# Second MLP product of the first two row chunks as seven block products, with the sums of the second weight matrix formed earlier

## The chip, the cores and the metric

The kernel runs on one NeuronCore of a Trainium2 chip. The engines that matter are PE (TensorE, matrix products), DVE (VectorE), ACT (ScalarE), POOL (GpSimd, which also issues a queue of DMA transfers) and SP (SyncE, which issues another). The metric is the device time of one execution in microseconds (us); lower is better. One execution was profiled, and its trace is what the times below are read from.

## The reference, cut to what matters

The program is an attention block followed by a Fourier mix with an MLP. Batch is 4, heads 8, sequence 768, head dimension 64.

```python
scores = scale * np.matmul(q, k.transpose(0, 1, 3, 2)) + bias   # bias: -slope * distance
scores = np.where(keep, scores, -1e9)                           # 8 global keys, 96 local keys
a = softmax(scores)
x = (a @ v) as (4, 768, 512)

X = np.fft.fft(np.fft.fft(x, axis=1), axis=2)
u = x + np.real(X)
un = (u - mean(u)) / np.sqrt(var(u) + 1e-6)
out = u + np.maximum(un @ w_ch1, 0.0) @ w_ch2                   # w_ch1 512x2048, w_ch2 2048x512
```

The change concerns the last product, `relu(...) @ w_ch2`. Its inner dimension is 2048 and its output has 512 columns.

## The kernel before, in words

**Tiling and stages.** The 3072 rows of the output are cut into twelve chunks of 256 rows, three to a batch: chunks 0, 1 and 2 are batch 0, and so on. For each batch the program does attention (scores `sc`, exponentials `ex`, the product with v, `pav`), divides by the row sums on DVE (`norm` at line 860, which writes the attention output `X[b]`), folds the sequence and the features with additions on DVE (`fold_s` and `fold_d`, lines 927 and 1086), does the remaining Fourier products on PE (`py`, `pu`), and adds and normalises on DVE and ACT (`u`, `un`). A chunk's normalised rows are transposed (`unT`; chunks 0 to 2 by PE as `ptu`, the others by DMA), then come eight groups of products with the first weight matrix (`ph`, eight matrix instructions each, line 1378), a ReLU into the hidden tile `hT` by ACT or DVE, and the second product.

**The second product, two forms.** Chunks 0 and 1 use `pg_unit` (line 1573): for each of the chunk's two blocks of 128 rows, sixteen matrix instructions of 512 columns add up in one PSUM bank `pg`, in four parts of four; DVE then multiplies by the row's 1/std and adds to `u` (line 1594). Chunks 2 to 11 use `pg_units` (line 1688): the 256 rows by 2048 inner by 512 columns are seen as 2x2 blocks times 2x2 blocks, and seven block products take the place of eight. A block product is eight matrix instructions of 256 columns (line 1697). They are issued as five pieces: p1 (one product), p45 (two), p6 (one), p7 (one) and p32 (two); the last chunk has six. p45 needs the first sum of the hidden tile, p6 the second, p7 the third and p32 the fourth. These four sums are made by DVE in `s_sums` (lines 1661, 1667, 1664 and 1672). Each piece is followed by one addition into `u` on DVE (line 1715), so a chunk has five of these where `pg_unit` has two.

**The sums of the second weight matrix.** The seven products also need sums of blocks of `w_ch2`, called W2T(0) to W2T(3). DVE makes them in `w2_sums` (line 1628), for i = 0 and 1, each with half the rows: `one` makes W2T(1) in the tile `misc` (line 1633), and `rest` makes W2T(3) in place, over a block of the weights themselves (line 1637), and then W2T(0) and W2T(2) in a tile `tt` (lines 1638, 1639). For i = 0 they read the first and third quarter of the weight rows, for i = 1 the second and fourth. Because W2T(3) overwrites weights that `pg_unit` reads, `rest` waits until chunks 0 and 1 are done (`pgdone`). The tile `tt` is also where batch 1's attention output stands (`XT`, line 837), so `rest` waits for that too. The constant `CS = 2` (line 410) says from which chunk on `pg_units` is used.

**Loads.** The weights come by eight transfers of 512 KB on POOL's queue, four for each matrix (`wload`, line 1883). The same queue loads q, k and v. Transfers of this queue use eight completion semaphores in turn, named DMASW0 to DMASW7 in the order rows below.

**What sets the order.** Each engine works through its instructions in program order. The order is written out by hand in the table `ORDER` (line 261), one list for each engine, of names such as G4 (a unit of the second product), H3 (a group of `ph`), M14 (a unit of the mix) or A43 (a unit of attention). A planner, `Plan`, walks these lists and issues the instructions; its `later` (line 87) records what an operation needs. The semaphore waits in the program follow from the tiles that are read and written. An operation whose input isn't there yet holds up all that stands behind it on its engine.

Of the kernel before, what the change touches and what calls it, by code (L numbers as in the profile page):

```python
# [12 lines left out]
ALU = mybir.AluOpType  # L13
# [11 lines left out]
class Plan:  # L25
# [135 lines left out]
    SHARED = {"kB": 1, "vB": 1, "sid": 1, "f1": 0, "f2": 0, "f3": 0, "z": 0, "g0": 0, "w": 0, "s": 0, "su": 0, "w2a": 0, "w2t": 0, "ex": 0}  # L161
# [78 lines left out]
    def unit_start(self, unit):  # L240
# [7 lines left out]
        if not there:  # L248
# [23 lines left out]
        ),  # L272
        "ACT": (
# [10 lines left out]
        ),  # L284
        "DVE": (
# [20 lines left out]
        ),  # L306
        "SP": (
            "T.6 T.0 T.9 T.127 T.35 T.133 T.10 T.128 G7.1 T.91 T.134 T.136 G3.1 T.137 T.130 T.100 T.131 T.101 T.176 T.182 T.102 T.177 T.185 T.34 T.206 "
            "T.183 T.140 T.186 T.212 T.205 T.211 T.179 T.149 T.180 T.263 T.150 T.151 T.222 T.223 T.228 T.189 T.229 T.198 T.199 T.200 T.245 T.239 T.240 "
            "T.246 T.258 T.256 T.257 "  # L310
        ),
    }
# [71 lines left out]
def kernel(  # L384
# [13 lines left out]
    Dm = H * Dh  # L398
# [1612 lines left out]
```

## Time and profile before

| | |
|---|---|
| time, median of 3 runs | 245.23 us (243.34, 245.23, 246.89) |
| the profiled execution | 244.25 us, of which 242.4 us lie between its first and last instruction (the span) |
| PE, matrix instructions | busy 230.6 us of the span, 3026 instructions |
| DVE | busy 206.4 us, 463 instructions |
| ACT | busy 143.3 us |
| POOL | busy 115.7 us |
| granted TensorE clock | 1.000 |

The 1.85 us between the profiled time and its span lie ahead of the first and behind the last instruction that was profiled. "PE" rows are matrix instructions and "PEld" rows the loads of their stationary operand, which overlap them. A row of the timeline gives the start, the duration, the engine, the line and operation, the tiles (written from read), how many, and in brackets how long the engine had been idle and what ended it. Durations of matrix instructions overlap, since they are pipelined: the start of one to the start of the next tells what a group costs.

### The profile page before, as it was taken

The page shows a single profiled execution, that of the slowest core. Times are in us where ns is not written, and L with a number is a line of the kernel's source. Part 1 is how long each engine was busy: PE and PEld are TensorE (multiplying, and loading weights), DVE is VectorE, ACT ScalarE, POOL GpSimd, SP SyncE. Part 2 cuts the span into 40 slices and gives each one's busy share as a digit, 9 for nine tenths or more (in the row PEclk, how much of TensorE's full clock was granted, in tenths as well). Part 3 has the DMA queues.
Part 4 walks back from the last instruction along what each step waited for, and adds up shares of the span by engine and source line. Part 5 has one row for each costly group of instructions (what it writes and reads, how often), then busy time and mean ns, then how long its engine had stood idle before and what let it go on. Part 6 is the DMA issues. An engine that isn't in the chain of part 4 may idle for free.

```text
span 242.4 us, 7226 instructions
## 1 busy us (share of the span) xinstructions
PE 230.6 (95%) x3026; PEld 188.2 (78%) x3026; DVE 206.4 (85%) x463; ACT 143.3 (59%) x233; POOL 115.7 (48%) x161
## 2 busy tenths in 40 slices
PE   7898899899999999889999999999999999999993
PEld 3465677598677668678988888898889899888882
DVE  3478997979961898999999899999998899988992
ACT  2288469974127978665268848845754588376300
POOL 8998769975800319999029854104140350003020
PEclk9999999999999999999999999999999999999999
DMA  7999999999999998999999956964892363103003
GB/s 181 166 164 180 203 209 193 206 207 168 129 159 178 206 182 66 136 178 96 133 220 294 200 76 192 177 32 87 252 271 46 78 141 66 25 0 143 34 26 147
DMA packets 103248, 35.44 MB, mean 146 GB/s; under 512 B 91088, under 2 KB 98640, under 8 KB 103216
## 3 DMA queue, kind: packets, MB, share of 16 engines
q0 software_dynamic: 72448, 19.16, 78.1%
q1 hardware_dynamic: 27216, 13.08, 25.6%
q10 hardware_dynamic: 3552, 2.75, 4.6%
q8 instruction: 23, 0.38, 0.6%
q14 instruction: 9, 0.07, 0.1%
HBM read 31.44 MB, written 8.65 MB: 165 GB/s over the span
## 4 chain that ended last, share of the span: by engine, by line
PE 77%; DVE 12%; ACT 4%; DMA 3%; issue 2%; POOL 1%; DVEq 0%; SPq 0%; POOLq 0%
PE ph L1378 22%; PE pgD L1697 14%; PE pgA L1697 10%; PE phA L1471 4%; PE py L1139 4%; PE pav L856 4%; PE pg L1583 4%; PE phX L1471 3%; DMA qkT<-qk 3%; ACT ex L800 3%; PE pu L1226 3%; PE pz L1860 2%; DVE x L868 2%; DVE ex L812 2%; PE sc L771 2%
## 5 line engine op out<-in xcount | busy, mean ns | idle before, releaser
L1378 PE MATMUL ph<-unT,w 128*128 128x256 f16 x576 | 71.4, 273 | 0.0
L1378 PEld LDWEIGHTS <-w 128*128 128x128 f16 x576 | 55.2, 98 | 8.4
L1383 ACT ACTIVATE hT<-ph 128x512 f16<-128x512 f32 x63 | 36.9, 596 | 41.7 <-PE ph L1378 41.4
L1697 PEld LDWEIGHTS <-hT 128*128 128x128 f16 x288 | 27.8, 98 | 4.8 <-issue 1.4
L797 ACT ACTIVATE er<-sc 128x1024 f16<-128x1024 f32 (+1 forms) x24 | 22.2, 951 | 10.0 <-DVE ex L812 6.0
L800 ACT ACTIVATE ex<-sc 128x1024 f16<-128x1024 f32 (+1 forms) x24 | 21.4, 959 | 8.5 <-PE sc L739 8.5
L1329 POOL TENSOR_SCALAR sm<-sm 128x2 f32<-128x2 f32 x12 | 5.2, 432 | 42.2 <-ACT un L1322 41.6
L1568 POOL DMA_INDIRECT out_dram<-u,back x4 | 5.4, 1345 | 30.7 <-DVE u L1715 30.4
L569 POOL DMA_DIRECT2D qk<-in_k_dram x16 | 13.5, 845 | 12.6 <-DMA qkT<-qk 8.4
L1715 DVE SCALAR_TENSOR_TENSOR u<-pgA,sm,u 128x256 f32<-128x256 f32 (+1 forms) x30 | 16.9, 565 | 1.5 <-PE pgA L1697 1.4
L1715 DVE SCALAR_TENSOR_TENSOR u<-pgD,sm,u 128x512 f32<-128x512 f32 (+1 forms) x21 | 15.0, 719 | 2.6 <-PE pgD L1697 2.5
L812 DVE TENSOR_TENSOR ex<-er,mk 128x1024 f16<-128x1024 f16 (+1 forms) x24 | 16.1, 688 | 0.0
L1583 PE MATMUL pg<-w,hT 128*128 128x512 f16 x64 | 15.5, 379 | 0.0
L1322 ACT ACTIVATE un<-un 128x512 f16<-128x512 f16 x24 | 15.0, 629 | 0.5 <-DMA unT<-un 0.5
L856 PE MATMUL pav<-v,ex 128*128 128x65 f16 x224 | 13.1, 193 | 1.9 <-DVE x L868 1.1
L856 PEld LDWEIGHTS <-ex 128*128 128x128 f16 x352 | 12.7, 97 | 2.8 <-issue 1.1
L569 POOL DMA_DIRECT2D qk<-in_q_dram x16 | 13.9, 879 | 0.0
L1152 ACT ACTIVATE zy<-py 128x1024 f16<-128x1024 f32 (+1 forms) x13 | 10.7, 825 | 4.3 <-PE py L1139 4.2
L868 DVE TENSOR_TENSOR x<-pav,rc 128x384 f16<-128x384 f32 x24 | 12.6, 554 | 0.6
L1384 DVE TENSOR_SCALAR hT<-ph 128x512 f16<-128x512 f32 x9 | 6.2, 685 | 7.1 <-PE ph L1378 7.0
L624 ACT ACTIVATE qk<-phA 128x512 f32<-128x512 f32 x12 | 6.9, 595 | 7.8 <-PE phA L1471 7.8
L1139 PE MATMUL py<-t,ww 128*128 128x256 f16 x80 | 11.2, 273 | 0.0
(217 smaller groups left out, 563.8 us busy)
## 6 DMA issues: line engine op xcount, KB each, us to landing
w<-in_moe_w_ch_dram POOLq DMA_DIRECT2D x8, 512.0 KB, 11.4
out_dram<-u SPq DMA_DIRECT2D x15, 256.0 KB, 3.5
v<-in_v_dram POOLq DMA_DIRECT2D x16, 192.0 KB, 7.0
qk<-in_k_dram POOLq DMA_DIRECT2D x16, 96.0 KB, 4.9
qk<-in_q_dram POOLq DMA_DIRECT2D x16, 96.0 KB, 5.0
xr<-xd SPq DMA_DIRECT2D x3, 512.0 KB, 4.0
xd<-x ACTq DMA_DIRECT2D x2, 768.0 KB, 5.3
ex<-w POOLq DMA_DIRECT2D x3, 512.0 KB, 6.7
```

The lines of the kernel that those rows point to most:

```text
L569: nc.gpsimd.dma_start(qk16[n][:, w, :, h], src[b, h0 + h].rearrange("(i m) d -> m i d", m=P))
L797: A(mine(), cut(pa), AF.Exp, 0.0, 0.125)
L800: A(cut(expst[hp][:, :, g * 512:g * 512 + (384 if g == 2 else 512)]), cut(pa), AF.Exp, 0.0, 0.125)
L812: VT(o, mine(), m, op=ALU.mult)
L856: nc.tensor.matmul(o[:, s * 65:(s + 1) * 65], lhsT, w, start=(a == 0), stop=(a == len(ops) - 1), skip_group_check=True)
L868: VT(X[b][:, 3 * (k.start + h):3 * (k.start + h) + 3, 2 * hp * Dh:(2 * hp + 2) * Dh].rearrange("p y (h d) -> p y h d", d=Dh), pv[:, h, :, ...
L1139: nc.tensor.matmul(o, lhsT, rhs, start=(x == 0), stop=(x == len(ops) - 1))
L1378: nc.tensor.matmul(ph[:, a * CH:(a + 1) * CH].rearrange("p (x m) -> p x m", x=2), W1[0][:, d, jb * P:(jb + 1) * P], UNT[c][:, :, d, :], st ...
L1383: pl.later([("ACT", act(512), lambda: A(dst, ph, AF.Relu)), ("DVE", dve(512), lambda: V.tensor_scalar_max(dst, ph, 0.0))], [], e, [("h", c ...
L1583: nc.tensor.matmul(pg, HT[c][:, jb, t * P:(t + 1) * P], W2[0][:, jb, :], start=(jb == 0), stop=(jb == NJ - 1))
L1697: nc.tensor.matmul(o, lhs(j), rhs(j), start=(first and j == 0), stop=(j == NK - 1), skip_group_check=True)
L1715: V.scalar_tensor_tensor(o, x, r(t), acc, op0=ALU.mult, op1=ALU.add)
```

## The change

Chunks 0 and 1 take the form with seven block products as well (`CS = 0`). Three things come with it.

- `w2_sums` is regrouped into three steps: `one` makes W2T(1), `middle` makes W2T(0) and W2T(2) from W2T(1) and unchanged weights, and `rest` makes W2T(3) in place. The eight additions are as many and as large as before. Nothing waits for `pgdone` any more, since no chunk reads the plain block.
- Batch 1's attention output stands in the tile `x`, where batch 0's stood, and the tile `tt` is free for the weight sums once the first loads of q and k that pass through it are used.
- The order table is new for all five engines. In it five ReLUs of `ph`, five normalisations `un`, three copies of transposed q and k (`qkT`) and two of `unT` go from DVE to ACT, and three of POOL's key copies (`kB`, in the tile `mk`) to DVE.

```diff
@@ Plan
-    SHARED = {... "w2a": 0, "w2t": 0, "ex": 0}
+    SHARED = {... "w2a": 0, "w2b": 0, "w2t": 0, "ex": 0}
@@ Plan.ORDER, "PE"
-... A44 H5 H4 A42 H1 A43 H6 M11 H0 H7 M13 G4 G0 H13 G5 G6 H9 H14 G1 G7 G2 H8 ...
+... A44 H3 A42 H7 A43 H6 H5 H4 M11 H2 H1 H0 H15 H12 H9 H8 G0 H10 H14 M13 H13 G1 M14 G2 H11 M15 G3 M18 G4 ...
@@
-    CS = 2
+    CS = 0
@@ w2_sums
+        def middle():
+            VT(W2T(0)[:, k0], W2[0][:, k0, 0:HC], W2T(1)[:, k0], op=ALU.add)
+            VT(W2T(2)[:, k0], W2[0][:, k1, 0:HC], W2T(0)[:, k0], op=ALU.subtract)
+
         def rest():
-            w = W2[0]
-            VT(W2T(3)[:, k0], w[:, k0, HC:Dm], w[:, k0, 0:HC], op=ALU.subtract)
-            VT(W2T(0)[:, k0], w[:, k1, HC:Dm], W2T(3)[:, k0], op=ALU.subtract)
-            VT(W2T(2)[:, k0], w[:, k1, 0:HC], W2T(0)[:, k0], op=ALU.subtract)
+            VT(W2T(3)[:, k0], W2[0][:, k0, HC:Dm], W2[0][:, k0, 0:HC], op=ALU.subtract)
         pl.later([("DVE", dve2(1024), one)], [("w2", 3), ("w2", 1)] + ..., [("w2a", i)], rank=2)
-        pl.later([("DVE", 3 * dve2(1024), rest)], [("w2a", i), ("pgdone",)] + free("tt", WTI), 0.0, [("w2t", i)], rank=2)
+        pl.later([("DVE", 2 * dve2(1024), middle)], [("w2a", i)] + free("tt", WTI), 0.0, [("w2b", i)], rank=2)
+        pl.later([("DVE", dve2(1024), rest)], [("w2a", i), ("pgdone",)], 0.0, [("w2t", i)], rank=2)
@@ pg_units
-        ws = [("w2t", 0), ("w2t", 1)]
+        ws = [("w2b", 0), ("w2b", 1)]
+        wt = [("w2t", 0), ("w2t", 1)]
-        PG.append((h1 + [("s", c, 1)] + ws, ..., p45))
+        PG.append((h1 + [("s", c, 1)] + ws + wt, ..., p45))
```

The order of instructions shows two places. The first is DVE, where batch 1's attention output is normalised (`rc` and the product behind it) and then folded (`eA`, `ww`, `zy`). Before, the fold follows the last normalisation:

```order
L866 RECIPROCAL rc_1_1_0_1241<-pav_1_1_1207 128x12
L868 TENSOR_TENSOR tt_1_1148<-pav_1_1_1207,rc_1_1_0_1241 128x3x128 x2
L866 RECIPROCAL rc_1_2_0_1280<-pav_1_2_1245 128x12
L868 TENSOR_TENSOR tt_1_1148<-pav_1_2_1245,rc_1_2_0_1280 128x3x128 x2
L1315 TENSOR_SCALAR un_2_1303<-u_4_1067,sm_2_1068 128x512 x2
L941 TENSOR_TENSOR eA_1_1318<-tt_1_1148 128x1536
L942 TENSOR_TENSOR eA_1_1318<-tt_1_1148 128x1536
```

In the changed kernel the same place reads as follows; the rows are given with the semaphores that an instruction waits for. The tile `w2_0` is the second weight matrix, `misc` holds W2T(1), and the lines are one or two later than before.

```order
L867 TENSOR_TENSOR x_1_1142<-pav_1_1_1169,rc_1_1_0_1204 128x3x128
L1632 TENSOR_TENSOR misc_73<-w2_0_663 128x1024 [waits DMAHW4_49,DMASW7_49,DMASW3_49]
L1632 TENSOR_TENSOR misc_73<-w2_0_663 128x1024 [waits DMASW2_49,DMASW0_49]
L1639 TENSOR_TENSOR w2_0_663<-w2_0_663 128x4x256 [waits DVE_49]
L865 RECIPROCAL rc_1_2_0_1259<-pav_1_2_1211 128x12 [waits PE_49]
L867 TENSOR_TENSOR x_1_1142<-pav_1_2_1211,rc_1_2_0_1259 128x3x128 [waits DVE_49]
```

Three of the eight weight sums (both of W2T(1), and W2T(3) for i = 1) now stand ahead of the last normalisation, and each W2T(1) sum waits for two transfers of POOL's queue. Behind the rows shown come the two sums of `middle` for i = 1, the first two instructions of the fold (`eA`), the two sums of `middle` for i = 0, more of the fold, and W2T(3) for i = 0.

The second place is POOL's list of transfers, where the weights are loaded (`w1_0` and `w2_0` are the two matrices, `qk` are rows of q and k for batch 2 on, `vB` copies of v). Before, the last weight transfer and its neighbours:

```order
L827 COPY vB1_88<-v161_85 128x528
L829 COPY vB1_88<-v161_85 32x528
L1173 COPY rev0_0_1048<-zy_1_903 128x2
L1174 COPY rev0_0_1048<-zy_1_903 128x2x127
L1175 COPY rev0_0_1048<-zy_1_903 128x256
L1893 DMA w2_0_847<-in_moe_w_ch2_dram 128x4x512
L569 DMA qk_4_1087<-in_k_dram 128x6x64
```

And in the changed kernel:

```order
L1890 DMA w1_0_769<-in_moe_w_ch1_dram 128x4x512 [waits DMASW5_49]
L568 DMA qk_2_1071<-in_k_dram 128x6x64
L568 DMA qk_2_1071<-in_q_dram 128x6x64 [waits DMASW7_49]
L1895 DMA w2_0_663<-in_moe_w_ch2_dram 128x4x512
L826 COPY vB2_89<-v161_85 128x528
L828 COPY vB2_89<-v161_85 32x528 [waits Pool_49]
L568 DMA qk_4_865<-in_k_dram 128x6x64 [waits DMASW1_49]
L1895 DMA w2_0_663<-in_moe_w_ch2_dram 128x4x512 [waits DMASW2_49]
L568 DMA qk_3_1208<-in_k_dram 128x6x64 [waits DMASW3_49]
```

Both lists have the same eight weight transfers, the last of them a quarter of the second matrix. Since the semaphores are used in turn, the two `w2_0` transfers shown are the ones that signal on DMASW0 and DMASW2, for which the second W2T(1) sum waits. Three of the `qk` loads that used to come behind all weights now stand ahead of the last, as shown, and a fourth further up, ahead of the last three transfers of `w1_0`.

More of the change, by code (lines that the diff above doesn't have):

```diff
@@ L159, in op_go @@
                 self.rings[ring].append((ring.e, ring.k))
-    SHARED = {"kB": 1, "vB": 1, "sid": 1, "f1": 0, "f2": 0, "f3": 0, "z": 0, "g0": 0, "w": 0, "s": 0, "su": 0, "w2a": 0, "w2t": 0, "ex": 0}
+    SHARED = {"kB": 1, "vB": 1, "sid": 1, "f1": 0, "f2": 0, "f3": 0, "z": 0, "g0": 0, "w": 0, "s": 0, "su": 0, "w2a": 0, "w2b": 0, "w2t": 0, "ex": 0}
     SLOW = ((0.56, 1.0, 1.0), (0.38, 0.7, 1.0))
@@ L262 @@
         "PE": (
[9 rows of a table removed]
[8 rows of a table added]
         ),
         "ACT": (
[10 rows of a table removed]
[10 rows of a table added]
         ),
         "DVE": (
[13 rows of a table removed]
[13 rows of a table added]
         ),
         "POOL": (
[5 rows of a table removed]
[5 rows of a table added]
         ),
         "SP": (
-            "T.6 T.0 T.9 T.127 T.35 T.133 T.10 T.128 G7.1 T.91 T.134 T.136 G3.1 T.137 T.130 T.100 T.131 T.101 T.176 T.182 T.102 T.177 T.185 T.34 T.206 "
-            "T.183 T.140 T.186 T.212 T.205 T.211 T.179 T.149 T.180 T.263 T.150 T.151 T.222 T.223 T.228 T.189 T.229 T.198 T.199 T.200 T.245 T.239 T.240 "
-            "T.246 T.258 T.256 T.257 "
+            "T.6 T.0 T.9 T.127 T.133 T.35 T.128 T.136 T.134 T.206 T.91 T.10 T.130 T.137 T.205 T.100 T.131 T.101 T.176 T.177 T.102 T.34 T.185 T.182 T.217 "
+            "T.140 T.186 T.223 T.216 T.183 T.222 T.179 T.149 T.180 T.276 T.150 T.151 T.233 T.234 T.189 T.240 T.239 T.198 T.199 T.200 T.257 T.251 T.250 "
+            "T.256 T.267 T.269 T.268 "
         ),
@@ L1790, in pg_units @@
         h1 = [("h", c, jp) for jp in range(4, 8)]
-        ws = [("w2t", 0), ("w2t", 1)]
+        ws = [("w2b", 0), ("w2b", 1)]
+        wt = [("w2t", 0), ("w2t", 1)]
         wd = [("w2", a) for a in range(4)]
         PG.append((h0 + wd + [("D",)], ("pg", "ph") if c >= NP * B - 2 else ("pg",), p1))
-        PG.append((h1 + [("s", c, 1)] + ws, ("pg", "ph") if c >= NP * B - 2 else ("pg",), p45))
+        PG.append((h1 + [("s", c, 1)] + ws + wt, ("pg", "ph") if c >= NP * B - 2 else ("pg",), p45))
         PG.append(([("s", c, 2), ("ra", c, 0)] + ws, None, p6))
```

73 rows, old and new, of the table ORDER are left out of this document.

## The prediction

> **What bounds the kernel now.** I read the page first, then the chain of waits, then windows, then the timelines of PE, DVE and POOL from 40 to 110 us.
>
> ```profile
> PE 230.6 (95%) x3026; PEld 188.2 (78%) x3026; DVE 206.4 (85%) x463; ACT 143.3 (59%) x233; POOL 115.7 (48%) x161
> PEclk9999999999999999999999999999999999999999
> PE 77%; DVE 12%; ACT 4%; DMA 3%; issue 2%; POOL 1%; DVEq 0%; SPq 0%; POOLq 0%
> ```
>
> PE carries 77% of the chain that ends last, DVE 12%, and the granted clock is full in every slice. The windows, and the two rows of PE behind them, show where PE is not the limit:
>
> ```profile
> 65.00:78.00 13.00, 13.00 (x98) 9.35 (x97) 5.95 (x13) 5.17 (x10) 0.54 (x1) 1.00 1.35 155
> 92.00:107.00 15.00, 13.21 (x221) 10.89 (x219) 14.83 (x25) 11.26 (x19) 14.62 (x19) 1.00 1.46 124
> ...
> 98.23 0.60 PE L1697 MATMUL pgD<-tt,hT 128*128 128x256 f16 x4 [1.10 <-DVE tt L1639]
> 106.81 0.20 PE L856 MATMUL pav<-v,ex 128*128 128x65 f16 x1 [0.62 <-DVE ex L812]
> ```
>
> The columns after the length are PE, PEld, DVE, ACT and POOL. From 65 to 78 us PE is full and DVE idles for 13.00 - 5.95 = 7.05 us; from 92 to 107 DVE is full, and PE waits twice, 1.72 us in all: chunk 2's p45 for the last weight sum, then an attention product. So in the middle of the kernel PE's time is the kernel's time: what shortens PE's work and opens no gap shortens the kernel, and a new gap of PE lengthens it.
>
> **Part 1: the products.**
>
> ```profile
> 61.83 1.73 PE pg L1583 x8
> 110.11 1.75 PE pgD L1697 x16
> L1583 PE MATMUL pg<-w,hT 128*128 128x512 f16 x64 | 15.5, 379 | 0.0
> ```
>
> In the chain, eight instructions of 512 columns cost 1.73 us, sixteen of 256 columns 1.75. The 64 old ones are eight such rows, 13.8 us; the new 2 x 7 x 8 = 112 are seven, 12.2 us. PE saves 1.6 us; the 48 more weight loads hide, as they do in chunks 2 to 11. The weight sums leave the full stretch of DVE at 92 to 107, so PE's 1.72 us there go as well. What would be late next there is DVE's other work; it has a margin, counted below. The sum of the gains is -3.3 us.
>
> **Part 2: DVE's load.** Two chunks add four sums of the hidden tile each, and ten additions into `u` replace four.
>
> ```profile
> L1667 DVE TENSOR_TENSOR sb<-eg,hT 128x1024 f16<-128x1024 f16 x6 | 4.1, 687 | 0.2
> L1715 DVE SCALAR_TENSOR_TENSOR u<-pgD,sm,u 128x512 f32<-128x512 f32 x19 | 14.1, 744 | 1.5 <-PE pgD L1697 1.3
> L1715 DVE SCALAR_TENSOR_TENSOR u<-pgA,sm,u 128x256 f32<-128x256 f32 x20 | 9.4, 476 | 1.2 <-PE pgA L1697 1.2
> L711 DVE COPY mk<-qkT 128x384 f16<-128x384 f16 x4 | 1.8, 445 | 0.1
> L704 DVE COPY qkT<-pt 128x1536 f16<-128x1536 f16 (+1 forms) x7 | 6.3, 894 | 4.3 <-ACT qkT L707 2.2 <-PE pt L680 2.1
> L1384 DVE TENSOR_SCALAR hT<-ph 128x512 f16<-128x512 f32 x9 | 6.2, 685 | 7.1 <-PE ph L1378 7.0
> L1315 DVE TENSOR_SCALAR un<-u,sm 128x512 f16<-128x512 f32 x17 | 8.5, 507 | 0.1
> ```
>
> Eight sums are 5.5 us. Of the additions, six more have 512 columns (4.5 us) and four have 256 (1.9), against four of 512 that go (3.0): +3.4. Three key copies come from POOL, at most 3 x 0.9 = 2.7 with twice the long part's price, at least 1.3. On ACT's side go three `qkT` copies (2.7), five ReLUs (3.4), five `un` (2.5) and two `unT` (at about a ReLU's size, 1.4): -10.0. The net is about +1 us of DVE over the whole kernel, which its 36 us of idle time cover; ACT has 99 us free. On balance I cost this at nothing. What matters is where DVE waits.
>
> **Part 3: a new wait on DVE, for a weight.** The second W2T(1) sum waits for the weight load that is last in POOL's list, and the last normalisation, the fold of batch 1 and the first sums of chunk 0 are queued behind it. When does that load land?
>
> ```profile
> 45.97 0.74 POOL L1893 DMA_DIRECT2D w<-in_moe_w_ch_dram  x1
> 52.95 0.82 POOL L569 DMA_DIRECT2D qk<-in_k_dram  x1 [0.87 <-DMA w<-in_moe_w_ch_dram]
> 55.44 0.82 POOL L569 DMA_DIRECT2D qk<-in_k_dram  x1 [1.66 <-DMA w<-in_moe_w_ch_dram]
> 57.97 0.82 POOL L569 DMA_DIRECT2D qk<-in_k_dram  x1 [1.72 <-DMA w<-in_moe_w_ch_dram]
> w<-in_moe_w_ch_dram POOLq DMA_DIRECT2D x8, 512.0 KB, 11.4
> qk<-in_k_dram POOLq DMA_DIRECT2D x16, 96.0 KB, 4.9
> ```
>
> Before, the last weight was issued at 45.97. POOL's waits at 52.95, 55.44 and 57.97 are each for the semaphore of the eighth transfer back, the last of them for just that load: it landed at 57.97. One 512 KB load landed every 2.5 us, so the queue is a pipe that was full until then. Four loads of 96 KB now stand ahead in it: 4 x 96/512 x 2.5 = 1.9 us. I take landing at R = 59.9. The lower bound is 57.9 (they cost nothing, or the order of the rest frees as much); the upper is 61.5, if the pipe runs empty for the 1.6 us that one more stop of POOL's list costs, such as those of 1.66 and 1.72 above.
>
> And when does DVE reach this sum? PE's part first:
>
> ```profile
> 48.52 0.37 PE L856 MATMUL pav<-v,ex 128*128 128x65 f16 x7
> 49.18 1.91 PE L1378 MATMUL ph<-unT,w 128*128 128x256 f16 x16
> 58.62 0.61 PE L1351 MATMUL ptu<-ident,un 128*128 128x128 f16 x8
> 59.07 1.89 PE L1583 MATMUL pg<-w,hT 128*128 128x512 f16 x8
> ```
>
> An attention product takes 49.18 - 48.52 = 0.66 us, a `ph` 0.87 (half of the sixteen above). The lists start alike, so I let both kernels begin at 48.52. The third product then ends at 48.52 + 3 x 0.66 + 2 x 0.87 = 52.2; its normalisation and the first W2T(1) sum make it 54.1. DVE so stands still for 59.9 - 54.1 = 5.8 us. The durations of what stands behind:
>
> ```profile
> 55.76 0.23 DVE L866 RECIPROCAL rc<-pav 128x12 f32<-128x12 f32 x1 [0.25 <-PE pav L856]
> ...
> 57.75 0.95 DVE L941 TENSOR_TENSOR eA<-tt 128x1536 f16<-128x1536 f16 x1
> ...
> 59.49 0.68 DVE L1384 TENSOR_SCALAR hT<-ph 128x512 f16<-128x512 f32 x1
> 60.09 0.68 DVE L947 TENSOR_TENSOR ww<-eA 128x1024 f16<-128x1024 f16 x1
> ...
> 62.37 0.68 DVE L967 SCALAR_TENSOR_TENSOR zy<-ww,eA 128x512 f16<-128x512 f16 x1
> ...
> 63.69 0.96 DVE L1095 TENSOR_TENSOR eA<-zy 128x1536 f16<-128x1536 f16 x1
> ...
> 65.62 0.95 DVE L1109 TENSOR_TENSOR eA<-zy 128x1536 f16<-128x1536 f16 x1
> ...
> 81.21 1.27 DVE L1633 TENSOR_TENSOR misc<-w 128x1024 f16<-128x1024 f16 x2
> ...
> 92.89 0.79 DVE L1637 TENSOR_TENSOR w<-w 128x1024 f16<-128x1024 f16 x1
> 93.71 1.00 DVE L1638 TENSOR_TENSOR tt<-w 128x1024 f16<-128x1024 f16 x1
> ```
>
> From R on: the W2T(1) sum 0.6 and W2T(3) 0.7; the normalisation 1.2 (0.23 and about 1.0); two sums of `middle` 1.3; the fold's first two rows 1.74 (57.75 to 59.49); two more sums 1.4: W2T(2) is complete at R + 7.0 = 66.9. Then 2.28 of fold (60.09 to 62.37), W2T(3) 0.7 and chunk 0's first sum 0.6: R + 10.6 = 70.5. Then fold again, 1.32 (to 63.69), one addition 0.4, and 1.93 (to 65.62): the inputs of the next `py`, M14, at R + 14.3 = 74.2.
>
> PE reaches chunk 0's p45 (G1) after four attention products, three `ptu` (0.45 each, 58.62 to 59.07), fifteen `ph` and p1: 48.52 + 2.6 + 1.35 + 16 x 0.87 = 66.4. It waits 0.5 for W2T(2), runs its first half to 67.8, waits 2.7 for the first sum (70.5), ends at 71.4, and waits 2.8 for M14's inputs. New waits: 6.0 us. This is the term that decides.
>
> The size of a weight sum is the one place where a page has another price. Beside POOL's copies two of them took 0.79 and 1.00 here, where the rows of 81.21 took 0.64 each. The Trainium skill, "SBUF — State Buffer", section "SBUF: two separate sides", says that a VectorE instruction with two SBUF inputs and a GpSimd one that reads SBUF exclude each other for a whole instruction. The slower rows agree. In the new place POOL has DMA issues and few copies, and by the page all six sums would then take 0.6 instead of 0.7, which would bring M14 forward by 0.6 us.
>
> **The sum.** 244.25 - 1.6 - 1.7 + 6.0 = 246.95 for an execution like the profiled one, whose 1.85 us around the span stay; the tail is the last chunk's and doesn't change. The median of before lies 0.98 above its profiled execution, so the forecast is 247.9.
>
> **The rivals.**
>
> *A, no wait.* The last weight lands early, since what shares the DMA engines with this queue has moved away and its loads go faster than 2.5 us each. With R of 54 the inputs of M14 are there at 68.3, when PE comes; p45 runs undisturbed and only the gains stay: 247.9 - 6.0 = 241.9; every us of R beyond costs one. For it: the eight loads took 11.4 us on average from issue to landing, far more than 2.5, so the rate hangs on what else is on the way. Against: three landings in even steps of 2.5 us, 4 us too late. Chance 0.18.
>
> *B, DVE doesn't catch up, slower.* Of the 7.05 us that DVE idled between 65 and 78, 5.8 are now spent ahead of them, and the sums and additions of chunks 0 and 1 (8.9 us) come due there and after. If DVE is still 1.5 us behind when PE comes to batch 2's first attention products, chunk 1's pieces and those products wait as chunk 2's did: 1.72 once more, at one more piece 0.62 as well, together +2.3: 250.2, and above with R at 61.5 (+1.6). For it: DVE is the fuller engine right there, 14.83 of 15. Against: the weight sums, six of them near 0.75 (4.5 us), have left that stretch, ReLUs too, and PE's own 6.0 us of waiting give DVE the same time. Chance 0.20.
>
> *C, the clock.* Two pauses of PE near 2.8 us could make the granted clock fall, and the groups behind them cost double until it is back: two to four groups of 0.87, +1.7 to +3.5, so 249.6 to 251.4. The longest pause of the middle is 1.10 us and the clock there 1.00; no row shows a longer one. Chance 0.05. The Trainium skill, "TensorE: Matmul & The Clock Gate", section "What's actually happening", has the clock at half after at least one idle window of about 3.4 us; the pauses I expect are shorter, and by that rule C doesn't occur.
>
> **How the numbers follow.** The forecast has what is left, 0.57. Its own range: R of 57.9 takes 2.0 off M14's start (245.9), R of 61.5 adds 1.6 (249.5); the three runs shown spread by 1.9 below and 1.7 above. The range reaches up through B and most of C, 251.5, and down to where A's upper half lies, 242.0; left out are A's lower half and the ends. A measurement of this kernel tells 2% from no change, 4.9 us here: faster is below 240.3, slower above 250.1. Faster takes a quarter of A: 0.05. Slower takes half of B and of C, and the top of the forecast, where R's upper bound and the runs' spread add up, 0.09: 0.21. The rest is 0.74.
>
> **What would show it.** In the timeline of DVE: an idle time of 5 to 7 us ahead of a W2T(1) sum at line 1632, ended by a weight load, at 59 to 61 us; the first sum of chunk 0 at about 70. In PE's: idle of 2 to 3 us inside chunk 0's first `pgD`, ended by `eg`, and as much ahead of a `py` near 74, ended by DVE; none near 98 and 107. The group of `pg` gone, and `pgD` and `pgA` 112 instructions longer together. Wrong, if line 1632 shows no idle time or its end is below 56 us (A), if PE waits for DVE beyond 100 us (B), or if a slice of the clock row is below 9 behind the pauses (C).

## The result, and the profile after

The changed kernel takes 251.28 us (median of six runs, 250.61 to 255.51), the kernel before 243.69 us (median of six). The ratio is 1.0279, 95% interval 1.0217 to 1.0341: 2.8% slower. Ratios here are those of mean times and leave out the executions of any kernel that fell into a slower state, so they differ a little from the quotients of the medians. The profiled execution took 251.28 us with a span of 249.5, against 244.25 and 242.4 before.

The page of the changed kernel, the lines on engines, on the granted clock, and on the chain that ended last:

```profile
PE 232.3 (93%) x3074; PEld 193.6 (78%) x3074; DVE 203.9 (82%) x459; ACT 158.1 (63%) x255; POOL 112.7 (45%) x157
PEclk9999999999977999999999999999999999999999
PE 50%; POOL 17%; DVE 13%; DMA 12%; ACT 3%; issue 3%; DVEq 0%; SPq 0%; POOLq 0%; ACTq 0%
```

Two things are new. PE holds 50% of the chain instead of 77%, and POOL and DMA, which had 4% together, have 29%: up to 61 us the chain runs mostly through POOL's list and the transfers (42 of 61 us), and from 98 to 148 us again in good part (28 us). And two slices of the clock row, from 69 to 81 us, are at 7.

The windows (PE, PEld, DVE, ACT, POOL, then the clock) show where it happened:

```profile
65.00:78.00 13.00, 7.92 (x51) 5.42 (x50) 12.68 (x26) 3.90 (x9) 0.23 (x1) 0.75 1.24 172
92.00:107.00 15.00, 15.00 (x231) 12.70 (x229) 14.28 (x38) 12.23 (x20) 9.63 (x14) 1.00 1.42 123
```

From 65 to 78 us the roles are changed: DVE, half idle there before, is full, and PE, full before, works 7.92 of 13 us, at a mean clock of 0.75. From 92 to 107, where PE lost 1.8 us before, it loses nothing. The timelines of DVE and then of PE around the place:

```profile
52.93 0.68 DVE L1632 TENSOR_TENSOR misc<-w 128x1024 f16<-128x1024 f16 x1
60.90 0.69 DVE L1632 TENSOR_TENSOR misc<-w 128x1024 f16<-128x1024 f16 x1 [7.29 <-DMA w<-in_moe_w_ch_dram]
61.51 0.68 DVE L1639 TENSOR_TENSOR w<-w 128x1024 f16<-128x1024 f16 x1
62.11 0.22 DVE L865 RECIPROCAL rc<-pav 128x12 f32<-128x12 f32 x1
63.30 0.68 DVE L1635 TENSOR_TENSOR tt<-w,misc 128x1024 f16<-128x1024 f16 x1
64.02 0.69 DVE L1636 TENSOR_TENSOR tt<-w,tt 128x1024 f16<-128x1024 f16 x1
...
70.57 0.68 DVE L1662 TENSOR_TENSOR eg<-hT 128x1024 f16<-128x1024 f16 x1
...
73.75 0.56 DVE L1096 TENSOR_TENSOR ww<-eA 128x768 f16<-128x768 f16 x1
```

```profile
67.83 1.03 PE L1698 MATMUL pgD<-tt,hT 128*128 128x256 f16 x8 [1.43 <-DVE tt L1636]
71.31 1.86 PE L1698 MATMUL pgD<-w,eg 128*128 128x256 f16 x8 [2.45 <-DVE eg L1662]
74.37 1.89 PE L1138 MATMUL py<-t,ww 128*128 128x256 f16 x8 [1.20 <-DVE ww L1096]
76.05 1.92 PE L1698 MATMUL pgA<-tt,sb 128*128 128x256 f16 x8
...
118.06 0.19 PE L855 MATMUL pav<-vB,ex 128*128 128x65 f16 x1 [1.02 <-POOL vB L828]
```

DVE stands still for 7.29 us ahead of the second W2T(1) sum until the last weight load lands at 60.8. What is queued behind it comes late, and PE pauses three times, 5.08 us in all: for W2T(2), for chunk 0's first sum, for the input of batch 1's first `py`. The groups of eight instructions from 71.31 on take nearly twice as long: 1.86 to 1.92 us where 1.03 is usual. Windows of 0.2 us give the times at which the clock changed, and one window of 3.4 us what PE did just before:

```profile
71.20:71.40 0.20, 0.09 (x1) 0.09 (x2) 0.20 (x2) 0.00 (x0) 0.00 (x0) 0.95 1.04 348
71.40:71.60 0.20, 0.20 (x2) 0.15 (x3) 0.20 (x1) 0.00 (x0) 0.00 (x0) 0.50 1.04 343
...
78.20:78.40 0.20, 0.20 (x3) 0.19 (x2) 0.20 (x2) 0.20 (x2) 0.11 (x2) 0.98 0.29 82
68.00:71.40 3.40, 0.95 (x9) 0.61 (x8) 3.40 (x9) 0.00 (x0) 0.00 (x0) 1.00 1.10 178
```

The clock fell to 0.50 at 71.4 and was back at 78.2, 6.8 us later. In the 3.4 us before the fall PE had been busy for 0.95 us.

The end differs too. The last stores on SP's queue, before and then after:

```profile
237.87 0.33 SPq L1816 DMA_DIRECT2D out_dram<-u  x1
238.97 0.81 SPq L1810 DMA_DIRECT2D out_dram<-u  x2
```

```profile
244.94 0.33 SPq L1812 DMA_DIRECT2D out_dram<-u  x1
245.31 0.43 SPq L1818 DMA_DIRECT2D out_dram<-u  x1
245.84 0.39 SPq L1812 DMA_DIRECT2D out_dram<-u  x1
```

Before, the store whose data are ready first goes first and the two others follow at once. After, it stands second, behind one that waits for the last matrix product. From the end of the last matrix instruction to the end of the span it is 242.4 - 238.42 = 3.98 us before and 249.5 - 244.39 = 5.11 after.

### The profile page after: what moved, and what is told of

Read it like the earlier page. It is cut to its first block, busy times and chain, and to the rows that moved or that the text cites. A ratio compares the mean times of both kernels' runs of the same rounds, so it can differ in the third digit from the quotient of the medians.

```text
span 249.5 us, 7339 instructions
## 1 busy us (share of the span) xinstructions
PE 232.3 (93%) x3074; PEld 193.6 (78%) x3074; DVE 203.9 (82%) x459; ACT 158.1 (63%) x255; POOL 112.7 (45%) x157
## 4 chain that ended last, share of the span: by engine, by line
PE 50%; POOL 17%; DVE 13%; DMA 12%; ACT 3%; issue 3%; DVEq 0%; SPq 0%; POOLq 0%; ACTq 0%
PE pgD L1698 12%; PE ph L1377 10%; PE pgA L1698 10%; POOL qk L568 4%; PE phA L1470 4%; DMA out_dram<-u 4%; DMA w<-in_moe_w_ch_dram 4%; DMA v<-in_v_dram 4%; PE phX L1470 3%; PE py L1138 3%; POOL vB L828 3%; POOL vB L826 2%; DVE u L1716 2%; PE pav L855 2%; PE pf L1046 2%
## 5 line engine op out<-in xcount | busy, mean ns | idle before, releaser
L1382 ACT ACTIVATE hT<-ph 128x512 f16<-128x512 f32 x68 | 40.3, 595 | 26.2 <-PE ph L1377 25.7
L1698 PEld LDWEIGHTS <-hT 128*128 128x128 f16 x352 | 33.8, 98 | 6.4 <-issue 2.0
L1328 POOL TENSOR_SCALAR sm<-sm 128x2 f32<-128x2 f32 x12 | 3.0, 252 | 58.7 <-ACT un L1321 58.3
L1716 DVE SCALAR_TENSOR_TENSOR u<-pgA,sm,u 128x256 f32<-128x256 f32 (+1 forms) x36 | 20.4, 566 | 4.2 <-PE pgA L1698 3.9
L1716 DVE SCALAR_TENSOR_TENSOR u<-pgD,sm,u 128x512 f32<-128x512 f32 (+1 forms) x25 | 18.0, 723 | 3.9 <-PE pgD L1698 3.8
L867 DVE TENSOR_TENSOR x<-pav,rc 128x384 f16<-128x384 f32 x32 | 16.7, 553 | 0.7
L1698 PEld LDWEIGHTS <-sb 128*128 128x128 f16 x128 | 12.8, 101 | 2.1
L826 POOL COPY vB<-v 128x528 f16<-128x528 f16 x14 | 9.7, 694 | 10.0 <-DMA v<-in_v_dram 10.0
L568 POOL DMA_DIRECT2D qk<-in_q_dram x16 | 13.5, 845 | 1.5 <-DMA w<-in_moe_w_ch_dram 1.3
L1698 PE MATMUL pgD<-tt,hT 128*128 128x256 f16 x88 | 11.4, 273 | 1.4 <-DVE tt L1636 1.4
L855 PE MATMUL pav<-vB,ex 128*128 128x65 f16 x128 | 10.1, 193 | 1.6 <-POOL vB L828 1.6
```

Of the source, the lines that this page charges most:

```text
L568: nc.gpsimd.dma_start(qk16[n][:, w, :, h], src[b, h0 + h].rearrange("(i m) d -> m i d", m=P))
L855: nc.tensor.matmul(o[:, s * 65:(s + 1) * 65], lhsT, w, start=(a == 0), stop=(a == len(ops) - 1), skip_group_check=True)
L867: VT(X[b][:, 3 * (k.start + h):3 * (k.start + h) + 3, 2 * hp * Dh:(2 * hp + 2) * Dh].rearrange("p y (h d) -> p y h d", d=Dh), pv[:, h, :, ...
L1382: pl.later([("ACT", act(512), lambda: A(dst, ph, AF.Relu)), ("DVE", dve(512), lambda: V.tensor_scalar_max(dst, ph, 0.0))], [], e, [("h", c ...
L1698: nc.tensor.matmul(o, lhs(j), rhs(j), start=(first and j == 0), stop=(j == NK - 1), skip_group_check=True)
L1716: V.scalar_tensor_tensor(o, x, r(t), acc, op0=ALU.mult, op1=ALU.add)
```

## The experiments

Theory 1 is the prediction's: DVE waits for the last weight load, and everything between 61 and 78 us follows from that. Theory 2: DVE has too much to do there, since the weight sums now stand ahead of the fold, and the wait only fills what would be slack. Theory 3 concerns the clock: it fell for another reason than PE's pauses.

**The wait taken away, order untouched (other_data).** For the half i = 0 the sums read the weight rows of the other half, which land earlier. This kernel's output is therefore not the reference's in what comes from those rows.

```diff
@@ w2_sums, for both i (i = 1 reads these rows anyway)
-            VT(W2T(1)[:, k0], W2[0][:, k1, HC:Dm], W2[0][:, k0, HC:Dm], op=ALU.subtract)
+            VT(W2T(1)[:, k0], W2[0][:, 12:16, HC:Dm], W2[0][:, 4:8, HC:Dm], op=ALU.subtract)
@@ middle: k0 and k1 replaced by 4:8 and 12:16 in the same way
```

> The changed kernel with its order untouched; only the first and third eighth of W2T(1), W2T(0) and W2T(2) (the half i = 0) are made from the weight rows of the other half, which landed earlier, so the second W2T(1) sum has nothing to wait for (that part of the output is not the reference's). Theory 1: DVE's idle time at that sum goes (from 7.3 us to under 1), the first py of batch 1 starts at 68 to 69.5 instead of 74.4, the clock stays full in this stage, and the time is that of fold_first, 243 to 245. Theory 2 (the order of DVE's work, with the weight sums ahead of the fold, is too slow by itself): the py starts after 71 and the time stays above 247.

Measured: 243.41 us, 0.9953 of before (0.9919 to 0.9987). Its timelines of DVE and of PE:

```profile
52.31 1.28 DVE L1632 TENSOR_TENSOR misc<-w 128x1024 f16<-128x1024 f16 x2
53.63 0.69 DVE L1639 TENSOR_TENSOR w<-w 128x1024 f16<-128x1024 f16 x1
```

```profile
65.62 1.04 PE L1698 MATMUL pgD<-tt,hT 128*128 128x256 f16 x8
66.49 1.04 PE L1698 MATMUL pgD<-w,eg 128*128 128x256 f16 x8
67.37 1.04 PE L1138 MATMUL py<-t,ww 128*128 128x256 f16 x8
...
93.42 1.92 PE L1377 MATMUL ph<-unT,w 128*128 128x256 f16 x16 [1.59 <-DMA unT<-un]
```

Both W2T(1) sums run back to back, p45 and `py` follow without a pause (`py` at 67.37, ahead of the 68 expected), and the kernel is a little faster than before. Nothing else in the order had to change, so theory 2 falls: taking one instruction's wait away brings back the whole loss.

**The wait taken away by order (fold_first).** On DVE, T.273 and T.270 are the two W2T(1) sums, T.275 and T.272 the W2T(3) sums, T.274 and T.271 `middle`, T.93 to T.98 the fold, A43.0 the last normalisation, T.201 and T.202 chunk 0's sums.

```diff
-A42.0 T.273 T.270 T.275 A43.0 T.274 T.93 T.271 T.94 T.272 T.95 T.201 T.96 G0.0 T.97 T.202 T.98
+A42.0 T.273 T.275 A43.0 T.274 T.93 T.94 T.95 T.96 T.97 T.270 T.271 T.201 T.272 G0.0 T.202 T.98
```

> The second W2T(1) sum, the two sums of the same half behind it and W2T(3) of that half stand behind batch 1's fold on DVE instead of ahead of the last normalisation; all else is the changed kernel. Theory 1 (DVE's wait for the last weight load is what made it slow): DVE comes to that sum at about 63.8 us, when the load is there, so its 7.3 us of idle time go; PE's three pauses (1.43, 2.45, 1.20) go but for 0.5 us at most, the clock stays at 1.00, and the time is 251.3 - 5.1 - 1.9 to 2.8 = 243.4 to 244.3. Theory 2 (DVE simply has too much to do between 53 and 80 us, the wait lay in slack): the pauses come back at the same three places and the time stays above 249.

Measured: 244.59 us, 1.0007 of before (0.9960 to 1.0054). The sum starts at 64.61 without waiting, `py` at 68.87, and the clock is full. In the profiled execution (246.73 us) PE has a new wait, the last of these rows:

```profile
64.61 0.68 DVE L1632 TENSOR_TENSOR misc<-w 128x1024 f16<-128x1024 f16 x1
...
68.87 1.04 PE L1138 MATMUL py<-t,ww 128*128 128x256 f16 x8
...
95.97 1.92 PE L1377 MATMUL ph<-unT,w 128*128 128x256 f16 x16 [2.54 <-DMA unT<-un]
```

PE now comes to chunk 3's `ph` before its transposed rows have landed. The same wait, 1.59 us, stands above in other_data.

**How much later per microsecond (qk_behind, late_w2).** The same kernel with the last weight load earlier and later.

```diff
@@ POOL, qk_behind: T.62 and T.64 are the last two weight loads, T.116, T.105, T.103, T.115 loads of q and k
-T.116 T.84 T.55 T.85 T.56 T.86 T.88 T.54 T.105 T.103 T.62 T.87 T.115 T.64 T.110
+T.84 T.55 T.85 T.56 T.86 T.88 T.54 T.62 T.87 T.64 T.116 T.105 T.103 T.115 T.110
@@ POOL, late_w2
-T.115 T.64 T.110 T.113 T.106 T.109
+T.115 T.110 T.113 T.106 T.109 T.64
@@ w2_sums, late_w2: the quarters that the sum reads, so that it is issued behind their loads
-..., one)], [("w2", 3), ("w2", 1)] + [...
+..., one)], [("w2", 3), ("w2", 1)] + [("w2", 0), ("w2", 2)] * (i == 0) + [...
```

> POOL's list with the four 96 KB loads of q and k behind the last weight load instead of ahead of it. Theory 1 with the queue as a full pipe: the last weight lands 1.9 us earlier (59.0 instead of 60.8), DVE idles 5.4 us instead of 7.3, PE's pauses are 1.9 us shorter, and the time is 249.4, or 247.5 if the clock stays full as well. Theory 2 (the wait lay in slack): 251.3. If the four loads cost nothing in the pipe: 251.3 too, with the landing at 60.8.

> The changed kernel with four more 96 KB loads of q and k ahead of the last weight load on POOL. If the queue is a full pipe of 512 KB per 2.5 us, each costs 0.47 us: the load lands at 62.7 instead of 60.8, the first py starts at 76.3 instead of 74.4, and the time is 1.9 us longer than that of the changed kernel, 253.2, more if the clock stays at half for another 3.4 us. If the landing is set by the issue on POOL instead (four issues of 0.83 us more): 64.1, py at 77.7, 254.6. If loads of q and k cost nothing: 251.3.

Measured: qk_behind 251.21 us (four runs from 248.14 to 254.08, too far apart for a ratio); late_w2 255.51 us, 1.0437 of before (1.0380 to 1.0494). DVE's sum in qk_behind, and PE's second product of p45 and first `py`:

```profile
59.91 0.69 DVE L1632 TENSOR_TENSOR misc<-w 128x1024 f16<-128x1024 f16 x1 [5.87 <-DMA w<-in_moe_w_ch_dram]
```

```profile
70.34 1.05 PE L1698 MATMUL pgD<-w,eg 128*128 128x256 f16 x8 [2.46 <-DVE eg L1662]
73.39 1.89 PE L1138 MATMUL py<-t,ww 128*128 128x256 f16 x8 [2.01 <-DVE ww L1096]
```

In late_w2 DVE's sum, POOL's issues of the last two weight loads, and PE (in the changed kernel these two were issued at 48.51 and 51.37):

```profile
65.89 0.69 DVE L1632 TENSOR_TENSOR misc<-w 128x1024 f16<-128x1024 f16 x1 [10.85 <-DMA w<-in_moe_w_ch_dram]
```

```profile
49.93 0.78 POOL L1895 DMA_DIRECT2D w<-in_moe_w_ch_dram  x1
...
56.11 0.76 POOL L1895 DMA_DIRECT2D w<-in_moe_w_ch_dram  x1
```

```profile
72.83 1.87 PE L1698 MATMUL pgD<-tt,hT 128*128 128x256 f16 x8 [4.99 <-DVE tt L1636]
76.32 1.89 PE L1698 MATMUL pgD<-w,eg 128*128 128x256 f16 x8 [1.62 <-DVE eg L1662]
79.38 1.89 PE L1138 MATMUL py<-t,ww 128*128 128x256 f16 x8 [1.17 <-DVE ww L1096]
```

The start of DVE's second W2T(1) sum and that of batch 1's first `py`, in all runs where the sum waited:

| kernel | sum | `py` | difference |
|---|---|---|---|
| qk_behind | 59.91 | 73.39 | 13.48 |
| fill_mid (below) | 60.80 | 74.28 | 13.48 |
| the changed kernel | 60.90 | 74.37 | 13.47 |
| the same again | 61.14 | 74.62 | 13.48 |
| fill_all (below) | 62.10 | 75.58 | 13.48 |
| late_w2 | 65.89 | 79.38 | 13.49 |

Whatever the landing, PE's `py` follows 13.5 us behind the sum. The landing moves PE one for one, and 5.0 us more of it cost about 4 us of time (255.51 against 251.28). The landing itself was forecast badly both times: four loads of 96 KB fewer ahead of it gave 1.0 us, not 1.9, and four more gave 5.0, not 1.9 or 3.3. In late_w2 the load was issued 4.7 us later (56.11 instead of 51.37) and took 9.7 us to land where it took 9.4. Of the 4.7, four more issues on POOL are 3.3, and 1.4 were already there at the weight load before it (49.93 instead of 48.51). So the later issue accounts for nearly all of the 5.0; but the queue also held more ahead of the load, and no run separates the two. Why qk_behind gave only half isn't settled; the landing itself varies by 1.3 us between runs of one order of transfers (60.7 to 62.0).

Qk_behind shows one thing more. With the four loads behind it, the last weight still lands at 59.8, against 57.7 in the kernel before (issued at 45.97, 11.7 us to landing). So those loads account for about 1.0 of the 3.1 us by which the landing moved; the rest comes from elsewhere in the new order. What the traces show there: by 40 us POOL had issued seven of the eight weight loads in the kernel before, and three in the changed kernel, where POOL then stood 5.67 us for DVE's `zy` and issued the other five from 40.87 to 51.37. No run tests that this is the reason.

**The clock (fill_all, fill_mid).** Spare matrix instructions, whose results are written over, stand where PE pauses.

```diff
@@ p45, for chunk 0 (fill_mid: only the second line, and none ahead of py)
+                spare(D_[:, 0:HC], 12)
             prod(D_[:, 0:HC], a(1, 1), tw(2), True)
+                spare(D_[:, HC:Dm], 20)
             prod(D_[:, HC:Dm], sx(0), tw(3), True)
@@ y_unit, for batch 1's first unit
+                for _ in range(18):
+                    nc.tensor.matmul(py[:, 0, 0:256], tab[:, 0, 0:128], tab[:, 0, 128:384], start=True, stop=True, ...)
```

> Spare matrix instructions of 256 columns, whose results are written over, fill PE's three pauses of the changed kernel: 12 ahead of chunk 0's p45, 20 between its two products, 18 ahead of the first py of batch 1. They add work that lies inside the pauses. Theory 1 (the pauses lower the clock): the granted clock is 1.00 from 71 to 78 us, the first py of batch 1 still starts near 74.4, since DVE sets that, and the time falls by the slow clock behind it, 0.8 + 0.8 + 0.25 = 1.9 us, to 249.4. Theory 3 (the clock fell for another reason): it is 0.5 from 71 to 78 as before, and the time stays at 251.3 or a little more.

> Only the middle pause of 2.45 us is filled, by 20 spare instructions; the other two stay. If the longest pause alone lowers the clock: clock 1.00 and 249.4, as with all three filled. If it is the idle share over some microseconds of all three: the other two still have 1.4 and 2.2 us of idle time but no stretch of 3.4 us is mostly idle, so the clock may stay full too; if it falls all the same, 251.3.

Measured: fill_all 250.08 us, 1.0201 of before (1.0085 to 1.0316); fill_mid 249.68 us, 1.0219 (1.0129 to 1.0309). The intervals reach over that of the changed kernel, so the stage decides. Windows of fill_all, then of fill_mid with its emptiest 3.4 us last:

```profile
68.00:72.00 4.00, 3.10 (x30) 2.64 (x27) 3.96 (x10) 0.10 (x2) 0.00 (x0) 1.00 1.05 206
72.00:76.00 4.00, 3.68 (x33) 2.77 (x30) 3.97 (x8) 0.00 (x0) 0.00 (x0) 1.00 1.22 151
```

```profile
68.00:72.00 4.00, 3.73 (x36) 3.09 (x33) 4.00 (x10) 0.25 (x2) 0.00 (x0) 1.00 1.03 216
72.00:76.00 4.00, 1.99 (x17) 1.22 (x15) 3.96 (x7) 0.00 (x0) 0.00 (x0) 1.00 1.05 189
...
70.90:74.30 3.40, 1.12 (x10) 0.73 (x10) 3.37 (x7) 0.00 (x0) 0.00 (x0) 1.00 1.12 200
```

With PE kept busy the clock stays at 1.00 through the stage while DVE is as late as ever, so theory 3 falls: the pauses lower the clock. All four profiled kernels that kept the pauses show the fall there (this one, its repetition, qk_behind, late_w2), and neither of the filled ones does. In fill_mid's profile filling the middle pause alone is enough. By the ratios the two fillings are worth 1.9 and 1.5 us, forecast was 1.9, with intervals wider than that. Both profiles lose clock in another place (below), which takes some of it back.

**The small ends, and a better order (fold_tail, fold_unt, fold_both, fold_all).** All start from fold_first.

```diff
@@ fold_tail, SP: T.269 is the store that is ready first; POOL: T.124 a copy of v (vB), six places earlier
-T.267 T.269 T.268
+T.269 T.267 T.268
@@ fold_unt: PE (M16 is pu of batch 1), DVE, ACT, SP (T.91 reads batch 1's rows)
-H20 H17 A51 A53 G6 M16 H21
+H20 M16 H17 A51 A53 G6 H21
-T.209 G6.0 A51.1 A53.1 M16.0 A45.1 M16.2
+T.209 M16.0 M16.2 G6.0 A51.1 A53.1 A45.1
-A51.0 H17.0 T.43 A53.0 T.46 A45.0 H18.0 M16.1
+A51.0 H17.0 M16.1 T.43 A53.0 T.46 A45.0 H18.0
-T.134 T.206 T.91 T.10
+T.91 T.10 T.134 T.206
@@ fold_both: both; fold_all: as fold_both, but
-A51 A53 G6 H21 (PE)      H17.0 M16.1 T.43 A53.0 T.46 (ACT)
+A51 G6 A53 H21 (PE)      H17.0 T.43 A53.0 M16.1 T.46 (ACT)
```

> fold_first with two small edits of the order: the last three stores on SP in the order in which their data are ready, as in the kernel before, and one copy of v on POOL (vB for heads of batch 2) four positions earlier. If the 1.15 us by which the changed kernel's end behind its last matrix instruction was longer comes from the order of these stores, the last store lands 0.5 to 0.7 us earlier; the copy takes a wait of PE of 0.3 to 1.0 us near 117 away where there is one (fold_first had none). Sum: 0.5 to 0.7 us faster than fold_first, 0.998 of before; if the tail is set by the transfers themselves: no difference.

> fold_first with the product pu of batch 1's first chunk (M16) 1.9 us earlier on PE, its additions and normalisation earlier on DVE and ACT, and the read of batch 1's rows (xr) ahead of two other transfers on SP. Theory: what ate the gain of the seven products in fold_first is PE's wait of 2.54 us near 96 us for chunk 3's transposed rows (unT), which hang on this chain; with the chain 2 to 3 us earlier the wait goes, and the time is 1.5 to 2.5 us below fold_first, about 0.992 of before. Rival: the wait was that one profile's (its transfer took 7.6 us where others take 4.3), and the time is that of fold_first, 1.00 of before.

> Both sets of edits on fold_first. If both work: 2 to 3 us below fold_first, 0.988 to 0.992 of before, which would be nearly the 3.3 us that the seven products and the weight sums were counted to save. If the gain of the products isn't there at all: 1.00 of before.

> fold_both with two moves that answer its own waits of 1.16 and 0.87 us for scores (PE waits for a bank that ACT empties): the scores A53 stand behind chunk 1's p45 on PE instead of ahead of it, and on ACT the copy of A53 stands ahead of the normalisation M16.1, which waited 1.44 us for DVE. If the seven products' gain is there behind these waits: 1.5 to 2.0 us below fold_both, 0.990 of before. If another wait takes their place at once: 0.998 as fold_both.

Measured, each against runs of the kernel before on its chip: fold_tail 0.9966 (0.9920 to 1.0012), fold_unt 1.0013 (0.9973 to 1.0052), fold_both 0.9978 (0.9949 to 1.0006), fold_all 0.9963 (0.9931 to 0.9995). Fold_unt, fold_both and fold_all were expected at 0.988 to 0.992 and missed it. SP's last stores in fold_tail, PE's new waits in fold_both, and fold_all's page:

```profile
240.16 0.33 SPq L1818 DMA_DIRECT2D out_dram<-u  x1
241.29 0.81 SPq L1812 DMA_DIRECT2D out_dram<-u  x2
```

```profile
83.63 0.37 PE L770 MATMUL sc<-qkT 64*32 64x128 f16 x18 [1.16 <-ACT er L796]
...
87.61 0.41 PE L770 MATMUL sc<-qkT 64*32 64x256 f16 x18 [0.87 <-ACT er L796]
```

```profile
PE 228.9 (95%) x3074; PEld 192.2 (80%) x3074; DVE 207.8 (86%) x459; ACT 158.1 (66%) x255; POOL 113.7 (47%) x157
```

With the stores in the order of their data, the part behind the last matrix instruction is 245.1 - 240.74 = 4.4 us in fold_tail, against 5.0 in fold_first: 0.7 us, as expected, though the total can't show that much. fold_unt took the wait for `unT` away and gave its gain to two new ones, for the scores' banks (1.16 and 0.30 us there, 1.16 and 0.87 in fold_both); fold_all took those away but for 0.33 us. It has the lowest ratio of the five orders tried here: 242.73 us, 0.4% below before with an interval that just clears no change, which as the best of several is weak evidence of a gain, and by the two ratios 3% below the changed kernel, by order alone.

**What PE's work is worth there (no_p6).** fold_all without one of the seven products in chunks 0 and 1; that part of the output is left out.

```diff
@@ p6
-            prod(A_[:, 0:HC], sx(1), tw(0), False)
+            if c > 1:
+                prod(A_[:, 0:HC], sx(1), tw(0), False)
```

> fold_all without the product p6 (eight matrix instructions of 256 columns) in chunks 0 and 1, so 16 of the 112 instructions and their part of the output are left out; all that DVE does stays. Prices the term on the products: if PE's time there is the kernel's time, the time falls by 2 x 0.87 = 1.7 us against fold_all, by which one of seven products is worth 0.87. If another engine sets the pace between 66 and 100 us: less than 0.5.

Measured: 244.36 us, 0.9966 of before (0.9921 to 1.0010): no gain over fold_all's 0.9963 can be seen, where 1.7 us (0.7%) were expected. Two waits of PE in its profile that fold_all hasn't:

```profile
83.25 0.41 PE L770 MATMUL sc<-qkT 64*32 64x256 f16 x18 [0.87 <-DMA qkT<-qk]
...
141.25 0.37 PE L770 MATMUL sc<-qkT 64*32 64x128 f16 x18 [0.97 <-DVE u L1291]
```

PE arrives sooner and waits for a transfer of q and k, later for DVE. So with the weight's wait gone, PE's work in chunks 0 and 1 is no longer all that sets the time.

**The changed kernel again (after_again).** No edit.

> The changed kernel once more, on the chip and beside the runs of fold_all. By theory 1 the same waits at the same places: DVE idle 6.5 to 8 us ahead of the second W2T(1) sum, PE's pauses of 4 to 5 us in all, the clock at half for 6.8 us from about 71, and 1.02 to 1.03 of before; fold_all is then 3 to 4% faster than it by an order alone.

Measured: 254.5 us (four runs from 250.16 to 257.21, too far apart for a ratio). In the profiled execution, 254.07 us, the sum waited 7.11 us, PE paused for 1.26, 2.45 and 1.17 us at the same three places, and the clock was at half for 10.2 us, from 69.9 to 80.1, where 6.8 from about 71 were expected.

## Why the prediction was right or wrong

The forecast was 247.9 us with a range of 242.0 to 251.5; the time is 251.28, at its upper edge. On record were a chance of 0.74 for a change within 2% and 0.21 for slower than that; the latter happened. That the time lies in the range, by 0.2 us, owes much to luck: the kernel before was taken as 245.23 and is 243.69 by the later runs, so that the forecast was an increase of 2.7 us and the measured one is 7.6; and the range was drawn up to 251.5 for two rivals with small chances.

- **The deciding term held in size, and its landing by luck.** Forecast: the load lands at 59.9, DVE stands still for 5.8 us, PE is at p45 at 66.4 and the first `py` starts at 74.2, with new waits of 6.0 us. Measured: 60.8, 7.29 us, 66.4 (67.83 - 1.43), 74.37, and 5.08 us of pauses. To these belong 0.83 us of the slow clock in p45's second half (1.86 - 1.03), which shorten the wait for `py`: 5.91 us together. The landing of 59.9 was worked out as 57.97 and 1.9 us for four loads of q and k. But 57.97 is when POOL went on, 0.3 us behind the landing at 57.7; the landing moved by 3.1 us, and by qk_behind those loads account for about 1.0; the other 2.1, for which the prediction had no term, come from the rest of the order. The path behind the sum took 13.47 us instead of 14.3; `py` started before the fold's last additions were through. The weight sums behind the wait took 0.60 (61.51 to 62.11) to 0.72 us (63.30 to 64.02) each, without POOL's copies beside them. So the lower price, which the prediction drew from the section "SBUF: two separate sides" of "SBUF — State Buffer" in the Trainium skill, was met by some of them and not by all; the 0.72 stands where the next instruction reads the sum just made. Of the two slower rows of the kernel before, only that of 1.00 us (from 93.71) ran beside POOL's copies (93.63 to 94.97); that of 0.79 ran almost wholly beside a DMA issue (92.53 to 93.62).
- **Rival C, the clock, was real, and had a chance of 0.05.** This is the step that failed: "the pauses I expect are shorter, and by that rule C doesn't occur". The prediction's own sign for C, a slice of the clock row below 9, is there. No pause was longer than 2.45 us, and the clock fell all the same, with 0.95 us of work for PE in the 3.4 us before. Three eights took 1.7, 1.7 and 1.1 us where 0.87 is usual; beside the 0.83 inside the wait this cost 0.81 + 0.83 + 0.24 = 1.9 us. The price in the text (1.7 to 3.5) was right, the condition wrong: a pause need not be 3.4 us long. That it takes several pauses together fits the runs, since the single pauses of 2.54 us in fold_first and 2.61 in fold_tail near 96 us left the clock at 1.00, but isn't shown. Here "TensorE: Matmul & The Clock Gate" of the Trainium skill ("What's actually happening") and the measurement differ, if "idle window" is read as a window without work: a partly idle stretch was enough.
- **Two terms were missing.** The end is longer by 1.13 us, which the prediction took as unchanged ("the tail is the last chunk's and doesn't change"); the order of SP's list is worth 0.7 of it by fold_tail, and the rest is open. A wait for a copy on POOL at 118, 1.02 us, and two small ones of 0.44 came with the new order; the copy's wait was 0.27 to 1.02 us in the six runs where DVE waited for the weight, and none in the others.
- **The sum closes.** 246.95 forecast for the profiled execution + 1.9 + 1.13 + 1.46 = 251.4 against 251.28. PE's waits ahead of 61 us, which the sum leaves out, differ by 0.6 us (5.8 before, 5.2 after), so it can't be trusted closer than that. The 0.98 us by which the median shown stood above the profiled execution were scatter: with the later runs the median of before is 243.69.
- **The products' saving came in PE's work and less in the time.** Fold_all's PE is busy for 228.9 us against 230.6: the 1.7 us are there. Its last matrix instruction ends 2.0 us earlier than before (236.45 against 238.42), of 3.3 forecast, and its end is 0.5 us longer. In time it is 0.4%, some 0.9 us: the term of -3.3 us was mis-sized wherever the weight's wait is gone. "What shortens PE's work and opens no gap shortens the kernel" is true by its second half, and gaps opened at once: for `unT`, for q and k, for DVE near 141.
- **Rival B didn't happen.** DVE caught up: PE is full from 92 to 107. **Rival A** is what other_data and fold_first show, at 243.4 to 244.6 instead of 241.9.

Why the order put the sum there can be read in the code, though no run tests it: the planner's list of what a W2T(1) sum needs (line 1640) names the quarters 3 and 1 for both halves, while the half i = 0 reads the quarters 0 and 2, the last two to be loaded. In the kernel before the sum stood at 81 us, where all had landed.

## What to carry to other kernels

When an operation is moved forward in an order, look up which loads it really waits for and when each landed, and count everything queued behind it on its engine; one early instruction cost 3% here, and moving it behind the fold gave them back. Count the loads issued so far at the same time in both kernels, and not only what stands around the last one. Count the slower clock behind pauses on the matrix engine even where each of them is short. And when the bound is relieved, go and see which waits sit just behind it before counting the gain.

## What the runs showed of the hardware that was not expected

The low clock comes in pieces of about 3.4 us: 6.8 us in the changed kernel and in qk_behind, 10.2 in late_w2 and in the repetition, and 3.4, from 11 to 12 us on, in fold_unt, no_p6, late_w2 and the fill runs, where the start of the kernel has pauses of up to 1.2 us. This early dip comes in some executions and not in others of much the same order. That fits windows that run free of the kernel, as the same section of the Trainium skill has it, with 3.4 us.

PE's share of work in the 3.4 us before doesn't tell by itself whether the clock falls. It fell behind 0.95 us of work in the changed kernel and behind 1.05 in qk_behind, and in the early dips of fill_all and fold_unt behind 1.62 and 1.94. It stayed at 1.00 behind 0.94 us of work in qk_behind (67.0 to 70.4 us) and behind 1.12 in fill_mid. Windows with a phase of their own would allow all of this; the runs don't show where they lie, so no threshold can be read from them.
